# Scores of two of eight groups per head as VectorE row dots in a fused decode-attention forward and backward kernel

## The chip, the cores and the metric

The kernel runs on one core of a Trainium2 chip. The metric is the device time of one execution in microseconds (us); smaller is better. The times before are the median of three runs, 1811.34 us (1810.82 to 1817.67).

## The reference

The reference is one transformer block in decode form (one query row per batch element) and its gradients with respect to all ten differentiable inputs. B = 2, H = 32 heads, 8192 cached keys of 128 elements per head, D = 512, F = 1376, all in bf16.

```python
mod = (_silu(c) @ w_mod).reshape(B, 6, 1, -1)           # sa, ca, ga, sb, cb, gb
h = _layernorm(x) * (1 + ca) + sa
q = (h @ wq) per head
scores = einsum('bhqd,bhkd->bhqk', q, k_cache) * Dh ** (-0.5)
o = einsum('bhqk,bhkd->bhqd', softmax(scores), v_cache)
x = x + ga * (o.reshape(B, 1, H * Dh) @ wo)
h = _layernorm(x) * (1 + cb) + sb
x = x + gb * ((_silu(h @ w1) * (h @ w3)) @ w2)
# outputs: x, and by jax.vjp with grad_out the gradients of
# x, k_cache, v_cache, wq, wo, w1, w3, w2, c, w_mod
```

The gradients of `k_cache` and `v_cache` are as large as the caches, 134 MB each, so that the core reads K once and V twice and writes two tensors of that size.

## The kernel before

The 64 pairs of batch element and head are called heads here. Each head's K and V are 2 MB: 128 partitions of 64 key blocks (`KK = 64`) of 128 elements. The blocks are handled in eight groups of eight (`NG = 8`, `GRP = 8`).

**Pass 1** (`job_a`), per head: K comes in two halves of 1 MB (`load_k`), V in one tile of 2 MB from the pool `big` or in two tiles of 1 MB from the pool `half` (`load_v`). `a_t` transposes a group's eight K blocks on TensorE into PSUM and copies them to an SBUF tile `kt`; the copy is ACT's for six groups and VectorE's for groups 2 and 6. `a_s` multiplies each turned block with the head's q column into one column of the score tile `S_ps` (64 columns). `a_max` takes the largest score of each partition on VectorE (L415), `a_bias` brings this to all partitions with a matmul and takes the minimum of the negated values (L424), and `a_exp` makes the exponentials on ACT. `a_scale` (L438, VectorE, four times per head) multiplies K by them into `ek`, into whose last column GpSimd copies the exponentials (L440). `a_m` makes 128 matmuls, 64 of V against `ek` (L453) and 64 of K against the exponentials (L455), and `a_evac` stores the results (L476 on ACT, L477 on VectorE).

**Pass 2** (`c_t`, `c_s`, `c_dv`, `c_ds`, `c_dk`), per head: V is loaded again and turned, dP comes from matmuls, and VectorE makes the two outer products (L997) that are written out by GpSimd's queue as gradients of K and V.

**Order.** The order is written out by hand in numbered slots: `at(slot, place, f)` registers a step, and at the end the slots are run in order, within a slot by place, where `PL_TASK` is last. Each engine's queue is in order. Head i of pass 1 starts at slot 8i: transposes of group g at slot 8i + g, its scores two slots later, the max at slot 8i + 10, the bias at 8i + 11, the exponentials at 8i + 12, the four scales at 8i + 13, 15, 17 and 19, the M matmuls at 8i + 15 to 8i + 22. So steps of three heads overlap.

The first 38 heads run without pass 2; this stretch is called pure pass 1. When head 31 is done, at slot `CS0` = 272, the output projection, the FFN and their backward of batch element 0 (`steps_chain`) run beside the heads that follow, one step in a slot. After that heads of pass 1 and pass 2 alternate, then the chain of batch element 1 follows, then pass 2 alone beside the weight gradients.

**d_hh**, the gradient at the FFN's hidden layer before the activation's part, is d_ffn times w2 turned; d_ffn depends on `grad_out` and `mod` alone. `steps_dhh` makes it by VectorE dots over rows of w2 (`dot`, L610, 11 per batch element), laid so that it ends shortly before `CS0`.

**Loads.** `want(need, kind, f)` registers a load with the slot in which it is needed. `pump` issues them on SP's queue strictly in that order, whenever the buffer that the first one wants is free: five `big` tiles of 2 MB, eleven `half` tiles of 1 MB, at most four V live. A load that finds no buffer holds up those behind it. One `big` tile is kept for the M results from head 0 on. `load_ffn` (w1 with half of w2, w3 with the other half) and `load_wo` take two `big` tiles each.

Of the kernel before, what the change touches and what calls it, by code (L numbers as in the profile page):

```python
# [8 lines left out]
BF16 = mybir.dt.bfloat16  # L9
F32 = mybir.dt.float32  # L10
ALU = mybir.AluOpType
# [7 lines left out]
def kernel(  # L19
# [26 lines left out]
    nc = tc.nc  # L46
    P = 128
    B, Sq, D = A_x.shape
# [15 lines left out]
    NG = KK // GRP  # L64
# [21 lines left out]
    ktp = ctx.enter_context(tc.tile_pool(name="ktp", bufs=5))  # L86
# [6 lines left out]
    def big():  # L93
        return bigp.tile([P, BIG], BF16, name="big", tag="big")
# [29 lines left out]
    qd = nc.sync  # L124
# [20 lines left out]
    K = {}  # L145
# [13 lines left out]
    def load_v(key, i):  # L159
        if free["big"] > 0:  # L160
            t = big()
            v = t[:, 0:KK * P].rearrange("p (k d) -> p k d", k=KK)
            qd.dma_start(v, src_of(A_v_cache, i))
            free["big"] -= 1
            V[key] = [v[:, 0:HK, :], v[:, HK:KK, :], "big"]
            return
        V[key] = []
        for hf in range(2):
            t = htile()
            qd.dma_start(t[:], src_of(A_v_cache, i)[:, hf * HK:(hf + 1) * HK, :])  # L170
            V[key].append(t)
        V[key].append("half")
        free["half"] -= 2
# [7 lines left out]
    def kb_(store, i, kk):  # L181
        return store[(i, kk // HK)][:, kk % HK, :]
# [141 lines left out]
    def at(slot, place, f):  # L324
        seq[0] += 1
        events.setdefault(slot, []).append((place, seq[0], f))
# [60 lines left out]
    def transposes(block, dve):  # L387
        tp = tps.tile([P, GRP, P], BF16, name="tp", tag="tp")
        for j in range(GRP):
            nc.tensor.transpose(tp[:, j, :], block(j), identb[:])  # L390
        kt = ktp.tile([P, GRP, P], BF16, name="kt", tag="kt")
        if dve:
            nc.vector.tensor_copy(kt[:], tp[:])  # L393
        else:
            nc.scalar.copy(kt[:], tp[:])  # L395
        return kt


    mstate = {}

    def a_t(i, g):
        if g == 0:
            S_ps[i] = head_ps()
        kts[(i, g)] = transposes(lambda j: kb_(K, i, g * GRP + j), g in (2, 6))

    def a_s(i, g):
        b, h = hb(i)
        kt = kts.pop((i, g))
        for j in range(GRP):
            cc = g * GRP + j  # L410
            nc.tensor.matmul(S_ps[i][:, cc:cc + 1], kt[:, j, :], qT_bf[:, h, b:b + 1], start=True, stop=True)  # L411
# [65 lines left out]
        nc.vector.tensor_copy(OK[:, i, :], m[:, P:P + 2])  # L477

    def job_a(i, s):
        for g in range(NG):  # L480
            at(s + g, PL_T, lambda g=g: a_t(i, g))
            at(s + g + LAG, PL_S, lambda g=g: a_s(i, g))
            at(s + g + MOFF, PL_M, lambda g=g: a_m(i, g))
            at(s + g + MOFF, PL_FREE, lambda g=g: a_free(i, g))
        at(s + NG + LAG, PL_MAX, lambda: a_max(i))
        at(s + NG + LAG + 1, PL_MAX, lambda: a_bias(i))
        at(s + NG + LAG + 2, PL_EXP, lambda: a_exp(i))
        for q in range(NQ):
            at(s + NG + LAG + 3 + 2 * q, PL_TT, lambda q=q: a_scale(i, q))
        at(s + MOFF + NG, PL_EV, lambda: a_evac(i))  # L490
# [29 lines left out]
    def load_ffn(a):  # L520
        t = big()
        free["big"] -= 1
        nm, ap = (("w1", B_w1), ("w3", B_w3))[a]
        wn[nm] = t[:, 0:NC * F].rearrange("p (k f) -> p k f", k=NC)
        qd.dma_start(wn[nm], ap.rearrange("(k p) f -> p k f", p=P))
        wn[("w2", a)] = t[:, NC * F:NC * F + F2 * D].rearrange("p (k d) -> p k d", k=F2)
        qd.dma_start(wn[("w2", a)], B_w2[a * F2 * P:(a + 1) * F2 * P].rearrange("(k p) d -> p k d", p=P))
        if a == 1:
            qd.dma_start(w2l[:FL, :], B_w2[(FC - 1) * P:F])
# [41 lines left out]
    bcp = ctx.enter_context(tc.tile_pool(name="bcp", bufs=1))  # L571
    BCW = 4 * P
# [6 lines left out]
    def spread_steps(put, vec, b, c0, c1, hold):  # L579

        st = {}

        def pe(c):
            if c == c0:
                st["t"] = bcp.tile([P, BCW], BF16, name="bc", tag="bc")
                hold["bc"] = st["t"]
            w = 0
            n = min(2, c1 - c)
            ps = scr(2 * P)
            for k in range(n):  # L590
                r = P if c + k < FC - 1 else FL
                nc.tensor.matmul(ps[:, k * P:k * P + r], vec[:r, c + k, b:b + 1].to_broadcast((r, P)),
                                 identb[:r, :r], start=True, stop=True)
                w = k * P + r
            st["ps"] = (ps, w)

        def ev(c):
            ps, w = st["ps"]
            nc.scalar.copy(st["t"][:, (c - c0) * P:(c - c0) * P + w], ps[:, 0:w])

        for c in range(c0, c1, 2):
            put(1, lambda c=c: pe(c))
            put(1, lambda c=c: ev(c))

    def dot(acc, w, vec):

        n = w.shape[-1]
        r = w.shape[0]
        junk = tps.tile([P, GRP * P // 2], F32, name="junk", tag="tp")
        nc.vector.scalar_tensor_tensor(junk[:r, 0:n], w, 1.0, vec, ALU.mult, ALU.mult,  # L610
                                       accum_out=acc)

    def steps_dhh(b):
        out = []

        def put(n, f):
            out.append((n, f))

        hold = {}

        def first():
            nc.vector.tensor_mul(d_ffn_bf[:, :, b], mod[:, 5 * NC:6 * NC, b], dy_col[:, :, b])

        put(1, first)
        spread_steps(put, d_ffn_bf, b, 0, NC, hold)
        for fc in range(FC):
            def f(fc=fc):
                r = fsz(fc)
                dot(d_hh[:r, fc, b:b + 1], w2_of(fc), hold["bc"][:r, 0:D])
            put(2, f)  # L630
        return out

    def turned_steps(put, groups, done):
# [245 lines left out]
    dh = [steps_dhh(b) for b in range(B)]  # L879
    ch = [steps_chain(b) for b in range(B)]  # L880

    def length(steps):
        return sum(n for n, _ in steps)
# [5 lines left out]
    CS0 = end_a(sA[H - 1]) + 1  # L889
    E0 = CS0 + length(ch[0])  # L890
    TC = E0 + 5
    FS0 = max(NG + 4, CS0 - length(dh[0]) - length(dh[1]) - 6)
    sC = []
    s = NG * H
    while len(sA) < NHD and s < TC:
        sA.append(s)
        s += NG

    na, ncc = NHD - len(sA), max(0, H - 1 - -(-(length(ch[1]) + 5 + MOFF) // NG))
    for k in range(na + ncc):  # L900
# [7 lines left out]
        sC.append(s)  # L908
        s += NG
    CS1 = end_a(sA[NHD - 1]) + 1  # L910
    lay(dh[1], lay(dh[0], FS0) + 1)
    lay(ch[0], CS0)
    for k in range(H // 2):
        lay(steps_do(0, k), E0 if k == 0 else max(E0 + 3 * k, sC[2 * k] - 10))
# [113 lines left out]
    for n in range(NHD):  # L1028
# [9 lines left out]

        want(s, "v", lambda n=n: load_v(("c", n), n))

    loads.sort(key=lambda x: (x[0], x[1]))


# [293 lines left out]
```

## Time and profile before

| | |
|---|---|
| median of 3 runs | 1811.34 us (1810.82 to 1817.67) |
| profiled execution | 1815.36 us, its span 1813.6 us, mean TensorE clock 0.782 |
| busy in the span | PE 1438.9 us (79%), weight loads 1336.8 (74%), VectorE 1183.5 (65%), ACT 953.5 (53%), GpSimd 333.4 (18%) |
| moved by DMA | 718.12 MB at 396 GB/s over the span |
| K halves, V tiles of 2 MB, V halves loaded | 128, 77 and 102 |
| written for the gradients of K and V | 256 transfers of 1 MB |

The profile is one execution recorded by the hardware. Its busy shares are means over the span; a second row of the page gives them in 40 slices of about 45 us, with the clock that TensorE was granted and the share of time in which the 16 DMA engines were busy. Other answers of the trace give one engine's instructions in order of time, groups of equal instructions with their mean duration, or sums over chosen stretches. A line such as L424 is a line of the kernel before. PE is TensorE, PEld its weight loads, DVE is VectorE, POOL is GpSimd, SP is the engine that issues the loads. Matmul and weight load overlap, and so do the ends of one VectorE instruction and the start of the next, so that the distance between two starts can be smaller than a duration.

### The profile page before, as it was taken

The numbers are of one execution on the slowest core, as the hardware profiler recorded it, in microseconds if no ns is written. First come the engines' busy times: TensorE is split into PE (matmuls) and PEld (weight loads), VectorE is DVE, ScalarE is ACT, GpSimd is POOL, SyncE is SP. The second block draws the span as 40 slices with busy tenths as digits, with TensorE's granted clock in tenths as the row PEclk, the third lists the DMA queues.
The fourth block names the chain that finished last, engine by engine and source line by source line (L and its number), as shares of the span: only waits on it lengthen the run. The fifth ranks groups of instructions, "written<-read, shape, count | busy, mean of one in ns | idle before, by whom it ended". The sixth has DMA issues, their size and how long they took to land. (4 is left out here: it accounts for less than half of the span.)

```text
span 1813.6 us, 60965 instructions
## 1 busy us (share of the span) xinstructions
PE 1438.9 (79%) x27266; PEld 1336.8 (74%) x27266; DVE 1183.5 (65%) x1687; ACT 953.5 (53%) x1362; POOL 333.4 (18%) x621
## 2 busy tenths in 40 slices
PE   6889999898987888778778888677877775866762
PEld 5888999898887878777777878677755563655662
DVE  2555556674676766766677667688775564565685
ACT  4555656553455454555455555343566574665751
POOL 0222222230121111211111112111121221111111
PEclk9999999996998787788777787766655565575775
DMA  9998998987899999999999999999999999999996
GB/s 384 421 421 344 386 386 321 415 316 291 305 381 420 413 414 425 408 410 418 416 412 418 412 410 409 404 415 406 408 418 410 414 412 426 420 421 415 404 423 289
DMA packets 99138, 718.12 MB, mean 396 GB/s; under 512 B 10128, under 2 KB 16988, under 8 KB 26300
## 3 DMA queue, kind: packets, MB, share of 16 engines
q1 hardware_dynamic: 57648, 430.00, 59.0%
q0 software_dynamic: 41216, 284.22, 37.6%
q8 instruction: 213, 3.49, 0.7%
q14 instruction: 49, 0.40, 0.1%
q10 hardware_dynamic: 12, 0.01, 0.0%
HBM read 429.99 MB, written 284.20 MB: 394 GB/s over the span
## 5 line engine op out<-in xcount | busy, mean ns | idle before, releaser
L395 ACT COPY kt<-tp 128x1024 bf16<-128x1024 bf16 x768 | 774.2, 1015 | 621.7 <-PE tp L390 606.5
L390 PE MATMUL tp<-identb,half 128*128 128x128 bf16 x5248 | 465.2, 240 | 29.1 <-issue 15.8
L390 PEld LDWEIGHTS <-half 128*128 128x128 bf16 x5248 | 356.0, 108 | 53.2 <-issue 39.4
L455 PEld LDWEIGHTS <-half 128*128 128x128 bf16 x4096 | 352.1, 96 | 7.8 <-issue 7.6
L393 DVE COPY kt<-tp 128x1024 bf16<-128x1024 bf16 x256 | 176.0, 688 | 241.0 <-PE tp L390 225.0
L390 PEld LDWEIGHTS <-big 128*128 128x128 bf16 x2944 | 240.6, 123 | 115.8 <-issue 115.0
L390 PE MATMUL tp<-identb,big 128*128 128x128 bf16 x2944 | 317.2, 273 | 5.7 <-DVE kt L393 2.9
L1002 POOL DMA_DIRECT2D out_dram<-half x256 | 136.3, 532 | 958.5 <-DVE half L997 716.3
L453 PE MATMUL m_ps<-ek,half 128*128 128x129 bf16 x2112 | 233.4, 228 | 17.7 <-DVE ek L438 14.7
L974 PEld LDWEIGHTS <-kt 128*128 128x128 bf16 x4096 | 190.6, 108 | 74.8 <-DVE kt L393 37.4
L974 PE MATMUL s_ps<-DO_bf,kt 128*128 128x1 bf16 x4096 | 192.6, 168 | 60.8 <-DVE kt L393 34.1
L411 PE MATMUL s_ps<-qT_bf,kt 128*128 128x1 bf16 x4096 | 178.7, 164 | 42.5 <-DVE kt L393 27.2
L453 PEld LDWEIGHTS <-half 128*128 128x128 bf16 x2112 | 198.7, 106 | 16.8 <-issue 16.1
L453 PE MATMUL m_ps<-ek,big 128*128 128x129 bf16 x1984 | 198.3, 217 | 4.4 <-issue 4.4
L411 PEld LDWEIGHTS <-kt 128*128 128x128 bf16 x4096 | 160.5, 98 | 49.4 <-DVE kt L393 29.4
L453 PEld LDWEIGHTS <-big 128*128 128x128 bf16 x1984 | 166.7, 96 | 5.3 <-issue 5.2
L1118 ACT CAST stg<-m_ps 128x512 bf16<-128x512 f32 (+2 forms) x123 | 72.6, 594 | 119.7 <-DMA out_dram<-stg 105.7
L1117 PE MATMUL m_ps<-big 2*128 2x512 bf16 (+2 forms) x123 | 72.5, 589 | 74.0 <-ACT stg L1118 71.9
L477 DVE COPY OK<-m_ps 128x2 f32<-128x2 f32 x64 | 10.0, 156 | 56.9 <-ACT big L476 56.9
L421 PE MATMUL s_ps<-nident,rm 128*128 128x128 bf16 x64 | 15.3, 238 | 40.0 <-DVE rm L415 40.0
L424 DVE TENSOR_REDUCE nm<-s_ps 128x1 f32<-128x128 f32 x64 | 18.4, 287 | 41.3 <-PE s_ps L421 41.3
L421 PEld LDWEIGHTS <-rm 128*128 128x128 bf16 x64 | 6.3, 99 | 42.1 <-DVE rm L415 42.1
(865 smaller groups left out, 2199.9 us busy)
## 6 DMA issues: line engine op xcount, KB each, us to landing
out_dram<-half POOLq DMA_DIRECT2D x256, 1024.0 KB, 15.8
big<-in_A_v_cache_dram SPq DMA_DIRECT2D x77, 2048.0 KB, 14.2
half<-in_A_k_cache_dram SPq DMA_DIRECT2D x128, 1024.0 KB, 11.6
half<-in_A_v_cache_dram SPq DMA_DIRECT2D x102, 1024.0 KB, 19.8
out_dram<-stg POOLq DMA_DIRECT2D x22, 512.0 KB, 21.2
big<-in_B_w_dram SPq DMA_DIRECT2D x4, 1376.0 KB, 12.1
big<-in_A_wq_dram SPq DMA_DIRECT2D x8, 512.0 KB, 13.1
big<-in_A_wo_dram SPq DMA_DIRECT2D x2, 2048.0 KB, 9.4
```

Source lines behind the costliest of these rows:

```text
L390: nc.tensor.transpose(tp[:, j, :], block(j), identb[:])
L393: nc.vector.tensor_copy(kt[:], tp[:])
L395: nc.scalar.copy(kt[:], tp[:])
L411: nc.tensor.matmul(S_ps[i][:, cc:cc + 1], kt[:, j, :], qT_bf[:, h, b:b + 1], start=True, stop=True)
L421: nc.tensor.matmul(s[:, KK:KK + P], kts.pop(("rm", i))[:].to_broadcast((P, P)), nident[:], start=True, stop=True)
L424: nc.vector.tensor_reduce(nm[:], s[:, KK:KK + P], AX.X, ALU.min)
L453: nc.tensor.matmul(m[:, 0:P + 1], vb_(V[i], kk), t[:, kk % QK, 0:P + 1], start=(kk == 0), stop=(kk == KK - 1), skip_group_check=True)
L455: nc.tensor.matmul(m[:, P + 1:P + 2], kb_(K, i, kk), E2[i][:, kk, 0:1], start=False, stop=(kk == KK - 1), skip_group_check=True)
L974: nc.tensor.matmul(DP[n][:, cc:cc + 1], kt[:, j, :], DO_bf[:, b, h:h + 1], start=True, stop=True)
L1002: sq_.dma_start(src_of(dst, n)[:, hf * HK:(hf + 1) * HK, :], t[:])
L1117: nc.tensor.matmul(ps[:lw, 0:rw], rsl(ln, lc, lw), rsl(rn, rc, rw), start=True, stop=True)
L1118: nc.scalar.copy(st["t"][:lw, o:o + rw], ps[:lw, 0:rw])
```

## The change

Three things are changed together.

First, for the heads of pure pass 1 in whole groups of four (`nv[0]` = 36: heads 0 to 35), groups 0 and 4 (`VG`) are no longer transposed. `a_spread`, once per four heads, brings the four q vectors to all partitions (four matmuls and an ACT copy into `qb`), and `a_dots` makes the eight scores of a group by eight `tensor_tensor_reduce` instructions on VectorE, each over one K block's 128 elements, whose sums go into the columns of `S_ps`. Their elementwise products go into a `kt` tile that nothing reads. The other six groups of these heads are all copied by ACT.

Second, d_hh is made by turning w2 on TensorE (`hh_steps`, in place of `steps_dhh`, `spread_steps` and `dot`), 44 transposes with six VectorE copies and 44 small matmuls, beside the fourth head (`HS0` = 24). w2 is loaded for it into a `big` tile of its own (`load_w2`), which is given back afterwards. The load of w1, w3 and w2 for the first chain is wanted at slot `CS0` - 1 instead of some slots before the old d_hh.

Third, the V of heads 0 to 35, where it goes to a `big` tile, is loaded in two transfers of 1 MB.

```diff
@@ load_v
-            qd.dma_start(v, src_of(A_v_cache, i))
+            if key == i and i < nv[0]:
+                for hf in range(2):
+                    ks = slice(hf * HK, (hf + 1) * HK)
+                    qd.dma_start(v[:, ks, :], src_of(A_v_cache, i)[:, ks, :])
+            else:
+                qd.dma_start(v, src_of(A_v_cache, i))
...
+    VG = (0, 4)
+    def a_spread(i0):
+        tp = tps.tile([P, GRP * P // 2], F32, name="qsp", tag="tp")
+        for n in range(4):
+            b, h = hb(i0 + n)
+            nc.tensor.matmul(tp[:, n * P:(n + 1) * P], qT_bf[:, h, b:b + 1].to_broadcast((P, P)), identb[:],
+                             start=True, stop=True)
+        t = cst_q.tile([P, 4, P], BF16, name="qb", tag="qb")
+        nc.scalar.copy(t[:].rearrange("p n d -> p (n d)"), tp[:])
+        qst["t"] = t
+    def a_dots(i, g):
+        junk = ktp.tile([P, GRP, P], BF16, name="kt", tag="kt")
+        for j in range(GRP):
+            cc = g * GRP + j
+            nc.vector.tensor_tensor_reduce(junk[:, j, :], kb_(K, i, cc), qst["t"][:, i % 4, :], 1.0, 0.0,
+                                           ALU.mult, ALU.add, S_ps[i][:, cc:cc + 1])
     def a_t(i, g):
         if g == 0:
             S_ps[i] = head_ps()
-        kts[(i, g)] = transposes(lambda j: kb_(K, i, g * GRP + j), g in (2, 6))
+        if g in VG and i < nv[0]:
+            return
+        kts[(i, g)] = transposes(lambda j: kb_(K, i, g * GRP + j), g in (2, 6) and i >= nv[0])
     def a_s(i, g):
+        if g in VG and i < nv[0]:
+            return
...
     def job_a(i, s):
+        if i < nv[0]:
+            if i % 4 == 0:
+                at(max(s - 2, 0), PL_TASK, lambda: a_spread(i))
+            for g in VG:
+                at(s + g, PL_TASK, lambda g=g: a_dots(i, g))
...
+    def hh_steps():
+        def tr(k):
+            tp = tps.tile([P, GRP, P], BF16, name="tp", tag="tp")
+            for n, f in enumerate(f for f in (2 * k, 2 * k + 1) if f < FC):
+                r = fsz(f)
+                src = w2e["l"][:r, :] if f == FC - 1 else w2e["t"][:, f, :]
+                for dc in range(NC):
+                    nc.tensor.transpose(tp[:, n * NC + dc, 0:r], src[:, dc * P:(dc + 1) * P], identb[:r, :r])
+            kt = ktp.tile([P, GRP, P], BF16, name="kt", tag="kt")
+            nc.vector.tensor_copy(kt[:], tp[:])
+        def mm(k):
+            for n, f in enumerate(fs):
+                for dc in range(NC):
+                    nc.tensor.matmul(ps[:r, n * B:(n + 1) * B], kt[:, n * NC + dc, 0:r], d_ffn_bf[:, dc, :],
+                                     start=(dc == 0), stop=(dc == NC - 1))
+                nc.vector.tensor_copy(d_hh[:r, f, :], ps[:r, n * B:(n + 1) * B])
...
-    FS0 = max(NG + 4, CS0 - length(dh[0]) - length(dh[1]) - 6)
+    HS0 = 3 * NG
+    nv[0] = len(sA) // 4 * 4
-    lay(dh[1], lay(dh[0], FS0) + 1)
+    lay(hh_steps(), HS0)
-        want(FS0 - 3 + a, "big", lambda a=a: load_ffn(a))
+        want(CS0 - 1 + a, "big", lambda a=a: load_ffn(a))
         want(CS0 - 3 + a, "big", lambda a=a: load_wo(a))
         want(CS1 + a, "big", lambda a=a: load_ffn(a))
+    want(HS0 - 1, "big", load_w2)
```

More of the change, by code (lines that the diff above doesn't have):

```diff
@@ L396, in transposes @@
         return kt
+    cst_q = ctx.enter_context(tc.tile_pool(name="qbp", bufs=1))
     mstate = {}
+    nv = [0]
+    VG = (0, 4)
+    qst = {}
+    def a_spread(i0):
[13 more added lines that the diff above has]
+                                           ALU.mult, ALU.add, S_ps[i][:, cc:cc + 1])
     def a_t(i, g):
@@ L527, in load_ffn, with load_w2 @@
         qd.dma_start(wn[("w2", a)], B_w2[a * F2 * P:(a + 1) * F2 * P].rearrange("(k p) d -> p k d", p=P))
-        if a == 1:
-            qd.dma_start(w2l[:FL, :], B_w2[(FC - 1) * P:F])
+    w2e = {}
+    def load_w2():
+        t = big()
+        free["big"] -= 1
+        w2e["t"] = t[:, 0:(FC - 1) * D].rearrange("p (k d) -> p k d", d=D)
+        w2e["l"] = w2l
+        qd.dma_start(w2e["t"], B_w2[0:(FC - 1) * P].rearrange("(k p) d -> p k d", p=P))
+        qd.dma_start(w2l[:FL, :], B_w2[(FC - 1) * P:F])
     def w2_of(fc):
@@ L570 @@
     dacc = cols.tile([P, NC, 2 * ((FC + 1) // 2)], F32, name="dacc", tag="dacc")
-    bcp = ctx.enter_context(tc.tile_pool(name="bcp", bufs=1))
-    BCW = 4 * P
     for z in (gate, up, d_hh):
@@ L577, in small @@
         return tmp.tile([P, n], F32, name=nm, tag=nm)
-    def spread_steps(put, vec, b, c0, c1, hold):
+    def hh_steps():
+        out = []
         st = {}
[L583 to L619, printed above, removed]
-        def first():
[L622 to L630, printed above, removed]
+        def first():
+            for b in range(B):
+                nc.vector.tensor_mul(d_ffn_bf[:, :, b], mod[:, 5 * NC:6 * NC, b], dy_col[:, :, b])
@@ new lines, in tr @@
+        def tr(k):
[6 more added lines that the diff above has]
+            kt = ktp.tile([P, GRP, P], BF16, name="kt", tag="kt")
+            if 2 * k + 1 < FC:
+                nc.vector.tensor_copy(kt[:], tp[:])
+            else:
+                nc.vector.tensor_copy(kt[:, 0:NC, 0:FL], tp[:, 0:NC, 0:FL])
+            st[k] = kt
@@ new lines, in mm @@
+        def mm(k):
+            kt = st.pop(k)
+            fs = [f for f in (2 * k, 2 * k + 1) if f < FC]
+            ps = scr(2 * B)
+            for n, f in enumerate(fs):
+                r = fsz(f)
+                for dc in range(NC):
+                    nc.tensor.matmul(ps[:r, n * B:(n + 1) * B], kt[:, n * NC + dc, 0:r], d_ffn_bf[:, dc, :],
+                                     start=(dc == 0), stop=(dc == NC - 1))
+                nc.vector.tensor_copy(d_hh[:r, f, :], ps[:r, n * B:(n + 1) * B])
@@ L631, in steps_dhh, with step, drop @@
+        def step(k):
+            if k < (FC + 1) // 2:
+                tr(k)
+            if k > 0:
+                mm(k - 1)
+        out.append((1, first))
+        for k in range((FC + 1) // 2 + 1):
+            out.append((2, lambda k=k: step(k)))
+        def drop():
+            w2e.clear()
+            release("big")
+            pump()
+        out.append((1, drop))
         return out
@@ L877, in lay @@
         return slot
-    dh = [steps_dhh(b) for b in range(B)]
     ch = [steps_chain(b) for b in range(B)]
```

## The prediction

> **What bounds the kernel now.** I read first the slices of the span (about 45 us each), where the last rows are the TensorE clock and the DMA engines:
>
> ```profile
> PE   6889999898987888778778888677877775866762
> DVE  2555556674676766766677667688775564565685
> PEclk9999999996998787788777787766655565575775
> DMA  9998998987899999999999999999999999999996
> ```
>
> From slice 12 on, about 545 us, DMA reads 9 throughout: the rest is bound by the bytes. Before it DMA dips and PE stands at 8 to 9. A second view sums chosen stretches (length, busy us and count of PE, weight loads, DVE, ACT, POOL, then clock, DMA share, GB/s):
>
> ```profile
> 40.00:160.00 120.00, 103.75 (x2470) 101.20 (x2467) 63.76 (x87) 64.59 (x86) 30.01 (x50) 1.00 0.99 409
> 160.00:320.00 160.00, 154.86 (x3732) 153.94 (x3733) 95.06 (x131) 95.81 (x131) 40.69 (x74) 0.99 0.92 359
> 320.00:410.00 90.00, 81.05 (x1939) 79.46 (x1937) 63.17 (x114) 50.70 (x71) 28.67 (x37) 1.00 0.92 364
> 410.00:500.00 90.00, 79.87 (x1753) 77.86 (x1751) 50.98 (x121) 36.66 (x53) 9.72 (x25) 0.85 0.78 298
> 560.00:1150.00 590.00, 479.51 (x9201) 465.07 (x9199) 407.29 (x526) 301.91 (x422) 104.88 (x211) 0.78 1.01 415
> ```
>
> From 160 to 320 us PE is busy 97% and DMA is not full: pure pass 1 is TensorE's there. After 560 DMA is full at 415 GB/s. So a microsecond won or lost before 500 us reaches the end unchanged, unless DMA fills sooner.
>
> The pace comes from the starts of L424, one per head: head 1 at 48.4 us, head 11 at 173.9, head 24 at 315.4, head 32 at 410.6. That is 12.5 us a head at first, then 10.9, then 11.9 while the w2 dots run. Heads 33 to 37 and the first FFN chain take 90 us more, to 500.5; pass 2's writes start at 495.
>
> [...] The change trades TensorE work for many short VectorE instructions, so their fixed cost decides. [...] the old w2 dots (L610) show both, and what two DVE ops cost with and without a wait between them:
>
> ```profile
> 341.57 1.25 DVE L438 TENSOR_TENSOR ek<-half,e_8738 128x2048 bf16<-128x2048 bf16 x1
> 342.74 0.69 DVE L610 SCALAR_TENSOR_TENSOR junk<-big,bc 128x512 f32<-128x512 bf16 x1
> 343.35 0.13 DVE L610 DVE_READ_ACCUMULATOR junk<-big,bc 128x1 f32 x1
> ```
>
> ```profile
> 425.43 0.18 DVE L710 CAST O_bf<-O_264 128x32 bf16<-128x32 f32 x1
> 425.52 0.18 DVE L711 SCALAR_TENSOR_TENSOR Qr_bf<-qT,rtot 128x32 bf16<-128x32 f32 x1
> ```
>
> ```profile
> 434.93 0.17 DVE L744 TENSOR_REDUCE lnst<-s_ps 128x2 f32<-128x8 f32 x1
> 435.13 0.17 DVE L745 TENSOR_SCALAR lnst<-lnst 128x2 f32<-128x2 f32 x1
> ```
>
> L711 needs nothing of L710 and starts 0.09 us after it; L745 waits for L744 and starts 0.20 after it, that is 0.03 after its end. [...] its copies L440 average about 500 ns from 160 to 320 us, but up to 896 ns beside the dots L610.
>
> **The change, part by part.** Numbers are for the profiled execution (span 1813.6, time 1815.4, which is 4 above the median of 1811.3).
>
> *Removed per head, heads 0 to 35:* 16 of 64 transposes and 16 of 64 score matmuls, 32 of 256 weight-load and matmul pairs. At 154.86 us for 3732 pairs a pair is 41.5 ns: 1.3 us of TensorE. The two DVE copies L393 of a head (691 ns, 0.61 start to start) go too, 1.2 us: the six groups left are all copied by ACT, as six were before.
>
> *Added per head:* 16 row dots of 128 elements on DVE. In the built program each is a multiply-reduce and an accumulator read, and each multiply-reduce carries a wait for the read just before it. The trace has no 128-element dot, so from L610: its read starts 0.61 to 0.62 us after it; [...] The read is 0.135, the wait's 0.03 follows: 0.385 us a dot, 6.15 us a head. *Lower bound* 0.25: the wait is free and the read hides as at L610, where the next op starts with it. *Upper bound* 0.46: [...] I take 0.385, since the program shows the waits.
>
> *DVE's cycle per head then:* four scales L438 at 1.13 start to start (the 1.219 ones overlap) 4.5; max 0.2; the wait for TensorE's bias matmul, 12.6 us for 15 heads in L424's row, 0.84; min 0.2; OK copy 0.1; dots 6.15: **12.0 us**. With upper bound dots it is 13.2, with lower bound 9.8. TensorE needs 10.9 less 1.3, 9.6, and DMA 4.19 MB at 415 GB/s, 10.1. DVE, which had 40% idle, becomes the bound. The waits that end last move: the bias matmul of a head waits for its max, queued on DVE behind the dots of the next head; and the first score matmul after each dotted group (groups 1 and 5) waits on TensorE for those dots, with the next transposes and M matmuls queued behind it. Both lie within one chain DVE to PE to DVE, so they add no more than the 0.84 counted.
>
> *Moved:* d_hh. Before, 22 dots (0.83 with the read) beside heads 24 to 31, where the pace was 11.9 to 12.9; that slowing goes. After, beside heads 3 to 6: 44 transposes, 44 small matmuls (88 pairs, 3.7 us, hidden in TensorE's new slack) and on DVE six copies (0.61) and 11 small ones (0.15), 5.2 us, not hidden. w2 is loaded once more, 1.4 MB, 3.4 us of DMA at 415 GB/s, issued at the start on SP between head 1's V and head 3's K; pass 1 then has DMA to spare at 349 GB/s (4.19 MB in 12.0 us): 0, and 3.4 if DMA were the bound.
>
> *Small:* a spread of q every fourth head (four matmuls, an ACT copy of 128x512; L1118's mean is 594 ns): 0.15 us of ACT a head, hidden, since ACT is busy 60%. V in two transfers: a further issue of about 0.4 us on SP, whose queue mostly waits for buffers: 0. GpSimd's copies at 0.9 us rather than 0.5, up to five a head: 4.5 of 12 us, and the M matmul that wants them comes four slots (6 us) after their scale: 0.
>
> *Sum for pure pass 1:* head 1 at 49, then 31 cycles of 12.0 (372) and 5.2: head 32 at about 426 instead of 410.6, +15. Heads 2 to 11 gain 6, heads 12 to 24 lose 15, the d_hh copies 5; heads 25 to 32 stand as before. Jitter between two engines that now wait for each other each head: I add 3 (0 to 10).
>
> *The first chain, heads 33 to 37:* DVE has 12.0 for each of heads 33 to 35 and 18 of chain ops (13 copies of 0.61, some 60 small ones), 54 us, beside 63 in which TensorE did them before; TensorE saves 96 pairs, 4 us. Each chain step stands behind up to 3 us of dots, and only part of that is covered: +5. The w1 and w3 loads now follow the wo loads at once, so four big buffers are wanted one after the other, each freed by one head; K's second half of head 34 is issued some 6 slots ahead of need, behind 2.7 MB of weights. Before, TensorE already waited 4.3 us for a K here. +2 (0 to 10). The clock was 0.85 from 410 to 500; [...]
>
> *After 500 us:* the same instructions, bound by bytes: 0. Sum: 15 + 3 + 5 + 2 = **+25**, so 1811 + 25, 1836.
>
> **Rivals.**
> *Faster, dots cheap.* If a dot costs 0.25 (the wait free, the read hidden), DVE's cycle is 9.8 and DMA or TensorE sets about 10.4. Head 32 comes at 49 + 31 x 10.4 + 5, 376, 34 earlier: **1780**. It decides below a cycle of 11.5 us, a dot of 0.36: there pass 1 breaks even. For it: TensorE at 97% really was the bound, and DVE was 60% busy. Against: each dot waits for its own predecessor.
> *Slower still, dots at 0.46.* A cycle of 13.2 gives head 32 at 463, +52, and 10 more in the chain: **1873**.
> *No difference:* dots about 0.36 and a chain helped by the clock: **1812**. For it: two thirds of the span are bound by bytes and untouched. Against: pass 1's loss has no later slack to be made up in.
> *The loads stall the chain* while pass 1 gains nothing: +10 to +20, **1826**, on the same side.
> The change does do what it says: the built program has these dots and fewer transposes.
>
> **How the numbers follow.** About 0.5% (9 us) is what a measurement of this kernel can tell from no change. Dots as worked out, with the load stall among them: 0.57; dots dearer: 0.15; no difference: 0.15; faster: 0.13. So slower 0.72, same 0.15, faster 0.13. The range 1800 to 1874 leaves out the cheap end of the faster case and the far end of the dear one.
>
> **What would show it.** Right: in the row of the dots about 0.2 to 0.3 us and reads of 0.13 us, starting 0.38 apart; DVE over 85% from 60 to 400 us; heads 12 us apart by the line of the min reduction; PE's largest named waits on DVE; DMA near 350 GB/s there. Wrong: DMA at 1.0 and 410 GB/s from 160 to 400 us, heads under 11 us apart, or heads unchanged and a new wait for K or big loads near the chain.

## The result, and the profile after

The kernel after takes **1922.69 us** (median of 4 runs, 1915.12 to 1929.36), the kernel before 1813.25 beside it (4 runs): a ratio of 1.060, interval 1.055 to 1.065. It is 109 us slower where 25 were forecast, and outside the range of 1800 to 1874. The profiled execution has a span of 1920.0 us, 106.4 above that of before, and a mean TensorE clock of 0.748.

The rows of the 40 slices (48 us each now: PE, VectorE, TensorE clock, DMA) show where:

```profile
PE   5777777787778888887788788878888778566862
...
DVE  4777767777666766676667766678876557466685
...
PEclk9788888888879878788877877766575556575766
DMA  9988777777659999999999999999999999999997
```

From the fifth slice to the twelfth, about 190 to 575 us, the DMA row reads 5 to 7; before, a single 7 was the lowest there. From the thirteenth on it reads 9, but for the last slice, as before. The TensorE clock, 9 in the first ten slices before, is now mostly 7 or 8 from the second slice on.

The same stretches as sums (length, busy us and count of PE, weight loads, VectorE, ACT, GpSimd, then clock, DMA share, GB/s):

```profile
160.00:320.00 160.00, 123.40 (x2487) 120.73 (x2487) 117.64 (x430) 75.34 (x103) 16.42 (x55) 0.85 0.74 292
410.00:500.00 90.00, 68.47 (x1401) 66.98 (x1400) 68.24 (x253) 42.38 (x57) 9.64 (x33) 0.87 0.72 274
620.00:1240.00 620.00, 508.75 (x9851) 492.69 (x9849) 427.03 (x551) 320.23 (x446) 110.22 (x222) 0.79 1.01 413
```

From 160 to 320 us **no engine is full**: PE 77%, VectorE 74%, DMA 74%. The pace over heads 11 to 24, by the starts of the min reduction (L456 now), is 14.55 us a head; it was 10.9. An engine that was the bound would have to be busy; three at three quarters suggest that they wait for each other. The third row is the stretch bound by bytes: clock, DMA share and rate stand as before.

Start of the min reduction of single heads, us:

| head | before | after | loss |
|---|---|---|---|
| 2 | 61.2 | 64.6 | 3.4 |
| 3 | 73.7 | 87.1 | 13.4 |
| 11 | 173.8 | 204.8 | 31.0 |
| 24 | 315.4 | 393.9 | 78.5 |
| 32 | 410.6 | 508.2 | 97.6 |
| 37 | 500.5 | 605.9 | 105.4 |
| 63 | 1145.2 | 1251.6 | 106.4 |

Pure pass 1 loses 97.6 us, the first chain 7.8, and all that follows 1.

**The wait that ends last.** Named waits from 160 to 320 us (engine, line, tile <- what released it: total us, times, longest), rows of VectorE and PE:

```profile
DVE OK L509 <- ACT big L508: 33.6, 11, 3.3
...
PE s_ps L443 <- DVE s_ps L426: 28.3, 11, 2.6
...
PE s_ps L453 <- DVE rm L447: 8.3, 11, 0.9
```

Eleven heads pass in this stretch, and each has one wait of each kind. TensorE waits 2.6 us a head at a score matmul (L443) for the dots (L426); VectorE waits 3.05 us a head at the small copy of the M results (L509), 33.6 over 11. Before, that copy (L477 there) waited 14.8 us in 14 heads, 1.06 each, and none of TensorE's named waits from 160 to 320 us was on VectorE:

```profile
DVE OK L477 <- ACT big L476: 14.8, 14, 2.0
```

How the two hang together is read from one head in order of time. First PE, then VectorE, then ACT (start us, duration us, engine, line, operation; in brackets the idle time before it and what ended it):

```profile
206.09 0.61 PE L395 MATMUL tp<-identb,half 128*128 128x128 bf16 x8
209.27 0.34 PE L443 MATMUL s_ps<-qT_bf,kt 128*128 128x1 bf16 x8 [2.57 <-DVE s_ps L426]
209.47 0.22 PE L485 MATMUL m_ps<-ek,big 128*128 128x129 bf16 x1
...
212.00 0.21 PE L487 MATMUL m_ps<-e_3689,half 128*128 128x1 bf16 x1
212.07 1.01 PE L395 MATMUL tp<-identb,half 128*128 128x128 bf16 x8
...
223.67 0.35 PE L443 MATMUL s_ps<-qT_bf,kt 128*128 128x1 bf16 x8 [2.56 <-DVE s_ps L426]
```

```profile
209.07 0.14 DVE L426 DVE_READ_ACCUMULATOR2_ANT s_ps<- 128x1 f32 x1
209.07 2.38 DVE L470 TENSOR_TENSOR ek<-half,e_3987 128x2048 bf16<-128x2048 bf16 x2
214.39 0.16 DVE L509 COPY OK<-m_ps 128x2 f32<-128x2 f32 x1 [2.93 <-ACT big L508]
214.50 0.29 DVE L426 CUSTOM_DVE_ANT_0 kt<-half,qb 128x128 bf16<-128x128 bf16 x1
...
219.18 0.29 DVE L456 TENSOR_REDUCE nm<-s_ps 128x1 f32<-128x128 f32 x1 [0.32 <-PE s_ps L453]
219.39 1.22 DVE L470 TENSOR_TENSOR ek<-half,e_3987 128x2048 bf16<-128x2048 bf16 x1
220.52 0.28 DVE L426 CUSTOM_DVE_ANT_0 kt<-half,qb 128x128 bf16<-128x128 bf16 x1
```

```profile
213.17 1.01 ACT L400 COPY kt<-tp 128x1024 bf16<-128x1024 bf16 x1 [0.91 <-PE tp L395]
214.08 0.27 ACT L508 CAST big<-m_ps 128x128 bf16<-128x128 f32 x1
```

The last dot of group 4 ends at 209.2 and the waiting score matmul starts at 209.27. It is not group 5's: it is the next one in TensorE's queue, **group 3's**, which writes into the same tile `S_ps` as the dots, in other columns. Group 4's dots stand at the end of slot 8i + 4, group 3's scores in slot 8i + 5, so they come directly after the dots. Behind that score matmul the last M matmuls (L485, L487) of the head two before are queued; they end at 212.21. ACT stores their result only at 214.08 (L508), because its own queue has the copy of the next group's transposes in front (L400, from 213.17), which TensorE turns after those M matmuls. VectorE's copy of the small part (L509, 214.39) comes after ACT's store, although both only read that tile, and this copy stands ahead of the next head's dots of group 0 (214.50) in VectorE's queue. These, a scale, the max, the bias matmul, the min (219.18), another scale and the dots of group 4 (from 220.52) follow one another, and at 223.67 the next score matmul is released. That is a **closed loop**: 5.1 us on TensorE and ACT (209.27 to 214.39) in which VectorE first finishes two scales and then idles 2.9, and 9.3 us on VectorE (to 223.67), in which TensorE runs out of work after some 7 us. Together 14.4 us, the pace.

The TensorE half of the loop is also slow in itself. Four short stretches around the stall:

```profile
206.70:209.20 2.50, 0.00 (x0) 0.00 (x0) 2.30 (x15) 1.01 (x1) 0.00 (x0) 1.00 0.88 364
209.30:210.10 0.80, 0.80 (x24) 0.80 (x24) 0.80 (x1) 0.00 (x0) 0.00 (x0) 1.00 0.12 51
210.10:213.50 3.40, 3.40 (x50) 3.40 (x49) 1.36 (x2) 1.34 (x2) 0.26 (x1) 0.50 0.17 29
213.50:216.90 3.40, 3.40 (x87) 3.40 (x85) 2.31 (x14) 1.98 (x4) 0.26 (x1) 1.00 0.91 364
```

The pause is 2.6 us long. When TensorE has been at work again for 0.8 us, the granted clock falls to 0.50 for 3.4 us: 50 matmuls where the next 3.4 us have 87. Up to ACT's copy at 213.17, two groups of eight transposes take 0.80 us each where they take 0.44 at full clock, and eight pairs of M matmuls 1.12 where they take 0.66; so about 1.2 us of the loop is the price of the stall itself. In the first experiment below, which has no such stall, the clock is 0.98 from 160 to 320 us. Each of the eleven stalls of 2.6 us from 160 to 320 us has such a stretch at 0.50, which begins between 0.9 us before the end of the stall and 1.5 us after it and is 3.4 us long eight times and 6.8 us three times.

### The profile page after: what moved, and what is told of

It reads as the page before. It is cut to its first block, busy times and chain, and to the rows that moved or that the text cites. A ratio compares the mean times of both kernels' runs of the same rounds, so it can differ in the third digit from the quotient of the medians.

```text
span 1920.0 us, 59992 instructions
## 1 busy us (share of the span) xinstructions
PE 1463.9 (76%) x26230; PEld 1359.5 (71%) x26230; DVE 1323.9 (69%) x2740; ACT 960.8 (50%) x1367; POOL 283.6 (15%) x621
## 4 chain that ended last, share of the span: by engine, by line
DMA 25%; issue 24%; DVE 22%; PE 21%; ACT 4%; POOL 3%; POOLq 0%; DVEq 0%; ACTq 0%; SPq 0%
DMA out_dram<-half 16%; PE m_ps L485 8%; PE tp L395 8%; DMA out_dram<-stg 8%; DVE kt L426 7%; DVE ek L470 5%; DVE half L1038 4%; ACT kt L400 3%; DVE s_ps L426 2%; POOL out_dram L1043 2%; PE s_ps L443 2%; DMA big<-in_w_mod_dram 1%; DVE kt L398 1%; POOL ek L472 1%; DMA big<-in_A_wq_dram 1%
## 5 line engine op out<-in xcount | busy, mean ns | idle before, releaser
L400 ACT COPY kt<-tp 128x1024 bf16<-128x1024 bf16 x768 | 774.3, 1015 | 698.7 <-PE tp L395 680.7
L395 PE MATMUL tp<-identb,half 128*128 128x128 bf16 x4672 | 445.8, 252 | 7.4 <-DMA half<-in_A_v_cache_dram 7.2
L487 PEld LDWEIGHTS <-half 128*128 128x128 bf16 x4096 | 365.7, 98 | 1.0 <-issue 1.0
L395 PEld LDWEIGHTS <-big 128*128 128x128 bf16 x2944 | 237.3, 122 | 110.9 <-issue 109.9
L395 PE MATMUL tp<-identb,big 128*128 128x128 bf16 x2944 | 312.8, 271 | 0.7 <-DVE kt L398 0.7
L443 PE MATMUL s_ps<-qT_bf,kt 128*128 128x1 bf16 x3520 | 154.4, 165 | 130.0 <-DVE s_ps L426 92.9
L1015 PEld LDWEIGHTS <-kt 128*128 128x128 bf16 x4096 | 190.4, 108 | 75.0 <-DVE kt L398 36.9
L443 PEld LDWEIGHTS <-kt 128*128 128x128 bf16 x3520 | 142.6, 100 | 139.8 <-issue 107.7
L485 PE MATMUL m_ps<-ek,half 128*128 128x129 bf16 x1984 | 225.7, 232 | 18.9 <-DVE ek L470 16.4
L485 PE MATMUL m_ps<-ek,big 128*128 128x129 bf16 x2112 | 237.1, 230 | 0.0
L398 DVE COPY kt<-tp 128x1024 bf16<-128x1024 bf16 x184 | 126.4, 687 | 153.8 <-PE tp L395 144.0
L485 PEld LDWEIGHTS <-half 128*128 128x128 bf16 x1984 | 192.7, 109 | 20.4 <-issue 20.3
L485 PEld LDWEIGHTS <-big 128*128 128x128 bf16 x2112 | 203.5, 108 | 0.4 <-issue 0.4
L426 DVE CUSTOM_DVE_ANT_0 kt<-half,qb 128x128 bf16<-128x128 bf16 x576 | 168.1, 292 | 19.5 <-ACT qb L419 1.2
L509 DVE COPY OK<-m_ps 128x2 f32<-128x2 f32 x64 | 10.0, 157 | 115.3 <-ACT big L508 112.2
L426 DVE DVE_READ_ACCUMULATOR2_ANT s_ps<- 128x1 f32 x576 | 80.7, 140 | 0.0
```

What stands on the lines that cost most here:

```text
L426: nc.vector.tensor_tensor_reduce(junk[:, j, :], kb_(K, i, cc), qst["t"][:, i % 4, :], 1.0, 0.0, ALU.mult, ALU.add, S_ps[i][:, cc:cc + 1])
L485: nc.tensor.matmul(m[:, 0:P + 1], vb_(V[i], kk), t[:, kk % QK, 0:P + 1], start=(kk == 0), stop=(kk == KK - 1), skip_group_check=True)
L487: nc.tensor.matmul(m[:, P + 1:P + 2], kb_(K, i, kk), E2[i][:, kk, 0:1], start=False, stop=(kk == KK - 1), skip_group_check=True)
L1015: nc.tensor.matmul(DP[n][:, cc:cc + 1], kt[:, j, :], DO_bf[:, b, h:h + 1], start=True, stop=True)
```

## The experiments

Two theories stood against each other. In one, the shared tile couples TensorE's queue to VectorE's and closes the loop above. In the other, the dots themselves are too dear: each waits for the read before it, and VectorE with its small waits is the bound, whatever TensorE does. Each run is compared with the kernel before on the same chip; its medians there were 1812 to 1817 us.

### Dots into a tile of their own, with and without waits between them

```diff
@@ a_dots
+        if g == VG[0]:
+            kts[("sd", i)] = hw.tile([P, len(VG), GRP], F32, name="sd", tag="sd")
+        sd = kts[("sd", i)]
-                                           ALU.mult, ALU.add, S_ps[i][:, cc:cc + 1])
+                                           ALU.mult, ALU.add, sd[:, VG.index(g), 0:1])      # with waits
+                                           ALU.mult, ALU.add, sd[:, VG.index(g), j:j + 1])  # without
@@ a_max
+            nc.vector.tensor_copy(S_ps[i][:, 0:KK].rearrange("p (h r) -> p h r", h=2)[:, :, 0:GRP], sd[:])
```

The sums go to an SBUF tile and are copied into the score tile just before the max. With all eight sums of a group in one column (broadcast to eight by the copy, so that seven of eight of these scores are left out) each dot still waits for the read before it. The copy line shown is the one without waits. Expected with waits:

> The dots' sums go to an SBUF tile of their own (each group's eight to one and the same column, so that each dot still waits for the read before it; seven of eight of these scores are therefore left out), and one small VectorE copy brings them to the score tile just before the max. TensorE's score matmuls then no longer wait for dots. Theory A (the lost time is a loop of waits: TensorE's first score matmul after a dotted group waits for the dots, the M matmuls behind it end late, VectorE's OK copy waits for them and holds up the next dots): the 2.9 us wait of the OK copy goes, heads come 12.2 us apart instead of 14.5, about 1845 us. Rival B (VectorE's busy time and TensorE's lower clock of 0.85 set the pace, the waits only show where it is spent): heads 13.5 to 14.5 apart, 1890 to 1920.

Expected without:

> As the run before it, but each dot has its own column of the SBUF tile; in the built program the waits between the dots are then gone too. If a wait costs what the trace after shows (0.39 us a dot with it, about 0.25 without), VectorE needs 9.9 us a head, and TensorE or DMA sets the pace: heads 10.4 to 11 apart, 1795 to 1810 us. If the waits between dots are free: as the run before it, 12.2 apart and 1845. Rival B: over 1880.

Measured with waits: **1804.46 us**, ratio 0.993 (0.990 to 0.997), 11.04 us a head. Against the kernel after, 118 us are gone, more than the whole loss, while every dot still waits for the one before: the second theory falls. The waits of VectorE in the same stretch:

```profile
DVE nm L463 <- PE s_ps L460: 6.0, 14, 1.2
DVE OK L516 <- ACT big L515: 2.4, 3, 1.1
```

The wait at the copy of the M results is 2.4 us where it was 33.6, and no wait of PE for dots is left. A dot into SBUF is also cheaper. VectorE in order of time, with waits and then without:

```profile
199.83 0.29 DVE L429 CUSTOM_DVE_ANT_0 kt<-half,qb 128x128 bf16<-128x128 bf16 x1
200.05 0.08 DVE L429 DVE_READ_ACCUMULATOR2_ANT sd<- 128x1 f32 x1
200.17 0.29 DVE L429 CUSTOM_DVE_ANT_0 kt<-half,qb 128x128 bf16<-128x128 bf16 x1
```

```profile
200.95 0.28 DVE L429 CUSTOM_DVE_ANT_0 kt<-half,qb 128x128 bf16<-128x128 bf16 x1
201.17 0.07 DVE L429 DVE_READ_ACCUMULATOR2_ANT sd<- 128x1 f32 x1
201.17 0.28 DVE L429 CUSTOM_DVE_ANT_0 kt<-half,qb 128x128 bf16<-128x128 bf16 x1
```

The read takes 0.08 us instead of 0.14 into PSUM, and the dots start 0.34 apart instead of 0.39. That is 0.8 us for the 16 dots of a head, some 29 us over 36 heads: it makes up most of the gap to the expected 12.2 us a head, and at most a quarter of the 118 us that are gone. Without the wait they start 0.22 apart, the next beginning together with the read.

Measured without waits: **1793.69 us**, ratio 0.986 (0.983 to 0.989), 10.90 us a head, and the bound has gone to DMA:

```profile
160.00:320.00 160.00, 139.78 (x3293) 137.00 (x3291) 126.68 (x582) 97.74 (x136) 24.06 (x72) 0.99 0.98 399
```

DMA is at 0.98 of its time and the TensorE clock at 0.99, where after had 0.74 and 0.85.

### The copy of the M results on ACT

This opens the loop at another place and leaves the shared tile: the copy no longer stands ahead of the dots.

```diff
-        nc.vector.tensor_copy(OK[:, i, :], m[:, P:P + 2])
+        nc.scalar.copy(OK[:, i, :], m[:, P:P + 2])
```

> The kernel after with the OK copy on ACT instead of VectorE, all else as it is. Theory A: VectorE no longer waits for the M matmuls, but TensorE still waits for the dots; the loop left is dots of group 4, five slots of TensorE (8.7 us in the trace after) to the last score, then max, min, a scale and the dots again (5.0): heads 13.0 to 13.7 apart, 1870 to 1895 us. Rival B: no change, 14.5 apart and 1915 to 1925.

Measured: 1885.16 us, ratio 1.037 (1.035 to 1.040), 13.17 us a head, as expected. The waits of PE and VectorE there:

```profile
PE s_ps L443 <- DVE s_ps L426: 33.1, 13, 2.6
```

```profile
DVE nm L456 <- PE s_ps L453: 21.5, 12, 2.3
```

TensorE still stalls 2.5 us a head for the dots. VectorE no longer waits at the copy, but now 1.8 us a head at the min instead of 0.3: the bias matmul stands behind the same stall. So both halves of the loop are as described, and its root is the wait over the shared tile. The runs moved the sums to SBUF; a second tile in PSUM, where the score tile lies, was not tried.

### The dots alone

The kernel before with nothing but `VG`, `a_spread` and `a_dots`, into the score tile; d_hh by the old dots, V in one transfer.

> The kernel before with the dots alone, their sums in the score tile as in the kernel after; the old d_hh dots and loads stay and V is loaded whole. Theory A (the loop of waits over the shared score tile carries most of the loss): heads 14.3 apart from head 6 to 24 as after, slower still beside the old d_hh dots; 1895 to 1920 us. If the w2 part and the V transfers carry as much as the dots: under 1870.

Measured: 1919.58 us, ratio 1.057 (1.055 to 1.059), 14.41 us a head. The dots carry the whole loss; the two other parts add 3 us to that, which is within the intervals.

### The other parts without the dots

```diff
-    VG = (0, 4)
+    VG = ()
-        kts[(i, g)] = transposes(lambda j: kb_(K, i, g * GRP + j), g in (2, 6) and i >= nv[0])
+        kts[(i, g)] = transposes(lambda j: kb_(K, i, g * GRP + j), g in (2, 6))
...
-            if i % 4 == 0:
+            if VG and i % 4 == 0:
```

> The kernel after without the dots: all eight groups turned again, groups 2 and 6 copied by VectorE as before; w2 turned beside the fourth head and V in two transfers stay. Theory A and rival B alike: heads 10.5 to 11.5 apart after head 11 as before; head 3 late by about 10 us (in the trace after SP sits 12 us on the small w2 load, and K of head 3 is issued 17 us later than before), and heads 25 to 31 faster by about 8 to 10 us in all without the old dots: 1805 to 1825 us. If w2 and the V transfers carry part of the loss for good: over 1830.

Measured: 1836.96 us, ratio 1.011 (1.008 to 1.014). This missed: 20 us slower than before with no dot in it, 12.58 us a head. The same with V in one transfer (`if key == i and i < nv[0]` made `if False`):

> The kernel after without the dots (all groups turned, copies as before) and with V in one transfer of 2 MB; of the change only the w2 part stays. The run without dots had heads 12.6 apart from head 11 to 24 where before has 10.9, with TensorE standing 0.65 to 0.85 us about every 6 us for nothing that the profile names. If the V transfers in two halves bring these stalls: 10.9 apart again and 1805 to 1820 us. If they come from what w2's early load leaves behind (fuller buffers, a shifted order of loads): 12.3 or more and 1830 to 1840.

Measured: 1834.47 us, ratio 1.010 (1.009 to 1.012), 12.22 us a head. The V transfers are not the cause; what is left of the change is the w2 part. With w2 turned beside head 14 instead of head 3 (`HS0 = 14 * NG`):

> No dots, V whole, w2 turned beside head 14 instead of the fourth: the w2 part alone at another place (beside the fourth: 1834.5 us, heads 12.2 apart from 11 to 24, TensorE standing 0.5 to 1 us about every 6 us some 2 us after a 16 KB piece of instructions begins to load). If w2's early load is what puts the loads and those stalls in step: heads 11 to 13 at 10.9 as before, and 1805 to 1820 us. If any shift of the loads does it: 12.2 and 1822 to 1836.

Measured: 1833.4 us, ratio 1.011 (1.008 to 1.014). The pace is 10.5 to 11.8 from head 11 to 13 and 12.3 after head 14's w2 part has passed. So something stays behind when that step is over, though it leaves no work. PE's idle time from 240 to 320 us in this run ends at matmuls that wait for nothing the profile shows ("issue"):

```profile
PE m_ps L487 <- issue: 5.9, 7, 1.3
PE m_ps L485 <- issue: 4.9, 6, 1.1
```

Thirteen pauses in 80 us, one about every 6 us. The page's row of the queue that brings instructions (packets, MB, share) reads

```profile
q8 instruction: 214, 3.51, 0.7%
```

which is 16.4 KB a packet. In the trace each of the thirteen pauses ends 2.2 to 2.6 us after the start of such a packet. How many TensorE instructions a packet holds is an estimate from such pages. That of the kernel before reads

```profile
PE 1438.9 (79%) x27266; PEld 1336.8 (74%) x27266; DVE 1183.5 (65%) x1687; ACT 953.5 (53%) x1362; POOL 333.4 (18%) x621
q8 instruction: 213, 3.49, 0.7%
```

With every packet counted as TensorE's, its 54532 matmuls and weight loads over 213 packets are 256.0 to a packet; after, 52460 over 205 are 255.9. By this estimate, a piece of 256 instructions to a packet, the 515 TensorE instructions of a head without dots are three more than two pieces, so the pieces end at nearly the same place in every head, and the w2 part moves that place (by 174 instructions in the trace). Counted so in the built program, the bias matmul of head 15 is instruction 237 of its piece before, and 155 in the run with w2 turned beside head 14. If the place matters, unread transposes (two instructions each) at the end of the w2 part bring the old pace back or not, depending only on their number:

```diff
+            left = 41        # or 105
+            while left:
+                tp = tps.tile([P, GRP, P], BF16, name="tp", tag="tp")
+                for j in range(min(GRP, left)):
+                    nc.tensor.transpose(tp[:, j, :], w2e["t"][:, left % 8, (j % NC) * P:(j % NC + 1) * P], identb[:])
+                left -= min(GRP, left)
```

With 41 the bias matmul is at 237 again:

> The run with no dots, V whole and w2 beside head 14 (1833.4 us; 10.5 to 11.8 a head up to head 13, 12.3 after), with 41 more transposes of w2 blocks that nothing reads at the end of the w2 part. They put TensorE's stream of instructions, which comes in pieces of 16 KB, back to the place in the head that it has in the kernel before (head 15's bias matmul is instruction 237 of its piece of 256, as before; without the padding 155). If the place of the piece's end within the head decides whether TensorE stands for its next piece: 10.5 to 11 a head after head 15, and 1808 to 1820 us although TensorE does more. If not: 12.3, and 1833 to 1840.

With 105 it is at 109:

> As the run before it with 105 such transposes: half a piece away from the kernel before (instruction 109). If the place decides: heads 12 or more apart after head 15, 1830 to 1842 us. If any padding helps, or none does, this run stands as the one with 41.

Measured: **1816.44 us** with 41 (ratio 1.001, 1.000 to 1.003) and **1834.12** with 105 (1.010, 1.007 to 1.013). From head 15 to 32 the pace is 12.3 us without padding, 11.1 with 41 and 12.0 with 105. PE's pauses in the same stretch, first with 41, then with 105:

```profile
PE s_ps L443 <- issue: 1.5, 2, 1.2
PE m_ps L485 <- issue: 0.6, 1, 0.6
PE m_ps L487 <- issue: 0.3, 1, 0.3
```

```profile
PE m_ps L485 <- issue: 3.2, 4, 0.9
PE s_ps L443 <- issue: 1.8, 3, 0.7
PE m_ps L487 <- issue: 1.7, 3, 0.8
```

Adding 41 idle transposes makes that kernel 17 us faster. By these rows the pauses come to 1.7 us a head without padding, 0.3 with 41 and 1.0 with 105, and the paces differ by about as much. So the three runs agree with the place where a piece ends within a head being what the w2 part changed, and with more and longer pauses for one place than for another. With dots a head has some 450 of these instructions, the place wanders from head to head, and in the kernel after no such pause is seen from 160 to 320 us; in the run with an own tile and no waits there are 23 there, 20 us together, while DMA sets the pace. That the pauses are TensorE waiting for such a piece is inferred from their distance to the packets and from these three runs; no record names it.

### Versions with the dots in their own tile

Own tile without waits, and in addition: w2 beside head 14; then V in one transfer too; then dots alone in the kernel before; and, apart from these, w2 early and one product and one row sum per group instead of eight dots.

> The kernel with the dots' sums in an SBUF tile of their own (1794 us), with w2's load and turning moved from slot 24 to slot 112 (beside head 14). If SP's 12 us on the small w2 load at the start delays head 3 for good: head 3 comes 10 to 13 us earlier, and 1781 to 1790 us. If DMA makes it up by the end of pass 1, or the stall only moves: 1792 to 1797.

Measured: 1786.64 us, ratio 0.984 (0.982 to 0.986), as expected. Head 3 comes at 66.8 us, where it came at 78.8 with w2 early. Some of this is lost again at head 14, which now comes 19.7 us after head 13. The reason for the late head 3 stands in the queue of the load engine in the kernel after (start, duration, line, what is loaded):

```profile
31.30 0.38 SPq L573 DMA_DIRECT2D big<-in_B_w_dram  x1
33.75 12.06 SPq L574 DMA_DIRECT2D w2l<-in_B_w_dram  x1
45.86 0.90 SPq L155 DMA_DIRECT2D half<-in_A_k_cache_dram  x2
```

The issue of the small second load of w2 held SP for 12.06 us, and head 3's K went out at 45.9 instead of 28.4 in the kernel before.

> The dots' sums in a tile of their own, w2 beside head 14, and V in one transfer of 2 MB instead of two (with two: 1786.6 us). The V transfers in halves let the first M matmuls start on half a V; with pass 1 near the bytes' bound (DMA share 0.96 to 1.01 with two) that is worth nothing: 1783 to 1791. If the halves help when DMA is full: 1793 to 1800.

Measured: 1790.82 us, ratio 0.988 (0.986 to 0.990). The intervals overlap with those of the run before it; what two transfers of V are worth is at most a few us, and its sign stays open.

> The kernel before with the dots alone, their sums in an SBUF tile of their own; the old d_hh dots beside heads 24 to 31, its loads and V whole. Heads 10.5 to 11 apart up to 24 as in the other kernels with such a tile; then VectorE carries 22 old dots of 0.83 us more, 18 us over eight heads, on top of 80% busy: heads 24 to 32 12 apart. 1785 to 1797 us. If the w2 part in truth only costs: under 1785.

Measured: **1786.53 us**, ratio 0.986 (0.983 to 0.988), 10.87 us a head, head 32 at 387.5 us. The dots alone, with their own tile, make the kernel before some 1.5% faster; this and the version with two V transfers and w2 at head 14 are the fastest of the runs.

> The kernel with the dots' sums in an SBUF tile of their own, with the eight dots of a group replaced by one product over 8 blocks (128x1024, bf16) and one sum of it by rows: 2 VectorE instructions for 16. [...] So VectorE's time stays, the waits stay, and so does the pace, 10.5 to 11 us a head: 1788 to 1800 us. If the many short instructions cost something more than their time (fetch, GpSimd's copies): under 1785.

Measured: 1790.33 us, ratio 0.987 (0.985 to 0.990). The two instructions of a group, VectorE in order of time:

```profile
202.71 0.69 DVE L428 TENSOR_TENSOR kt<-half,qb 128x1024 bf16<-128x1024 bf16 x1
203.43 1.22 DVE L430 TENSOR_REDUCE sd<-kt 128x8 f32<-128x1024 bf16 x1
```

1.94 us from the start of one to the end of the other, little more than eight dots of 0.22 without waits (1.76), and the same total: with DMA full, this choice no longer decides. That VectorE's time would stay was the author's estimate.

## Why the prediction was wrong

**The dot: right.** 0.385 us was forecast; in the kernel after the dots start 0.39 apart, with a read of 0.14. The multiply-reduce's share of the forecast was the author's estimate; in the trace after the read starts 0.22 us after it.

**VectorE's cycle: this step failed.** The prediction saw that a score matmul would wait on TensorE for the dots with M matmuls queued behind it, and put this at nothing: the bias matmul and the score matmul "lie within one chain DVE to PE to DVE, so they add no more than the 0.84 counted". VectorE's own busy time is 10.7 us a head (117.64 over 11), near the 11.2 that the sum of 12.0 has without that wait. But the cycle came to 14.55, because the wait is not within the sum: TensorE's leg of 5.1 us from the released score matmul to the copy L509 runs mostly while VectorE waits, 3.05 us a head there where 1.06 was the measure of before. Two things were missed: that the waiting matmul was group 3's, one slot after the dots, with M matmuls behind it (groups 1 and 5 had been named; group 1's scores, three slots after group 0's dots, wait for nothing); and that the M results' small copy stands ahead of the dots in VectorE's queue, which closes the loop. Head 32 was put 15 us later, and came 97.6 later.

**The clock: missed in pass 1.** The forecast's sum has no term for it. In the first chain it is 0.83 (508 to 606 us) where it was 0.85 (410 to 500 us before), so the chain gained nothing from it. In pass 1 the stalling TensorE got 0.85 from 160 to 320 us where it had 0.99. This is part of the loop's TensorE leg, about 1.2 us a head.

**The w2 part: two costs missed, neither decisive.** The prediction gave SP and DMA nothing; the issue held SP 12 us and head 3 came late, 12 us later than with w2 at head 14; in the whole time this was 7 us with the own tile (1793.69 against 1786.64), and the intervals overlap. And the shift of the instruction pieces was not thought of: 17 to 20 us without dots for the w2 part, of which the padding brought back 17 with w2 at head 14; none seen beside the loop.

**V in two transfers, GpSimd: right at 0.** GpSimd's copies were even shorter, 0.30 us (16.42 over 55), not the 0.9 feared.

**The chain and what follows: right in size.** +7 forecast for the chain, 7.8 measured; 0 after it, 1 measured. The 7 were 5 for the dots of heads 33 to 35 and 2 for the loads; no run takes these apart, and the dots of these heads write into the shared tile too, so the agreement may be luck.

**The rivals.** The faster one needed dots under 0.36 us to break even; the kernels without the loop fit that: with 0.34 and an own tile 1804, with 0.22 1794 to 1787. The slower one, 1873, had dots of 0.46, the author's estimate and a wrong cause. The rival that was missing is a wait through a shared tile.

**The signs to look for.** "DVE over 85%" came out at 74%, and DMA at 292 GB/s instead of about 350: both fit that no single engine is the bound, which the forecast had no case for. PE's largest named wait was on VectorE, as forecast.

**Heads 3 to 10 of the kernel before**, which ran at 12.5 us, show the same pauses of TensorE. From 75 to 160 us there:

```profile
PE tp L390 <- issue: 7.8, 9, 1.2
PE s_ps L411 <- issue: 2.8, 3, 1.1
```

These are 10.6 us in some seven heads, 1.6 each; from 160 to 320 us they are 5.2 us in fifteen, 0.4 each. That is 1.2 of the 1.6 us by which the pace changes. By the estimate of 256 to a piece, and counted back from head 15's 237 with three instructions a head, their bias matmuls are at 201 to 222; over heads 15 to 32 the slow run with w2 beside head 14 has 155 to 206, the fast padded one 237 and more. But DMA was also full there (0.98), so whether the place or the full DMA brings the pauses stays open. Open as well is how the own tile's gain splits into the cheaper read and the lost coupling, beyond the estimate of 29 us above.

## What to carry to other kernels

When an engine begins to write into a tile that another one also writes, look at which instruction of the other is next in the queue for that tile, and what is queued behind it, before adding up busy times: two in-order queues that waited for each other once per round cost the sum of their legs here, 5.1 and 9.3 us, and the sign was that no engine was full. Here it helped to give the sums an SBUF tile of their own and to join them late. In the long unrolled stream here, 41 transposes more that nothing depends on moved the time by 1% (1833.4 to 1816.44 us), probably through where the 16.4 KB pieces of instructions end; repeat a small difference with a padded control before giving it a cause.

## What was not expected of the hardware

- A row dot of 128 elements takes 0.39 us from start to start into PSUM with a wait, 0.34 into SBUF with a wait and 0.22 without. The wait costs 0.12 us a dot there.
- TensorE ran at half clock for 3.4 us after a pause of 2.6 us; each of the eleven such pauses from 160 to 320 us has 3.4 or 6.8 us at half clock about its end.
- 41 transposes that nothing reads made a kernel 17 us faster, 1816.44 us against 1833.4; 105 did not, 1834.12. The likely reason, inferred and named by no record, is the place within the head where a 16.4 KB piece of instructions ends.
- The issue of a small load behind a large one held the load engine's queue for 12 us.
